# Sliding-window attention and a multiplicative feed-forward network on one core: two weight matrices multiplied on chip, and an attention of one key block per query block, placed by hand

## The chip, the core and the metric

One core of a Trainium2 chip runs the whole program. The metric is the device time of one execution in microseconds (us), as the median of several runs. Engines are named as the profile names them: PE (TensorE; PEld are its weight loads), DVE (VectorE), ACT (ScalarE), POOL (GpSimd) and SP (SyncE). Each engine works through its own instructions in order and waits on semaphores for the others.

## What is computed

```python
B, H, S, D = 8, 8, 576, 64
scores = (1 / sqrt(D)) * q @ k.transpose(0, 1, 3, 2)       # q, k, v: [B, H, S, D]
rel = pos[:, None] - pos[None, :]
# heads 0 to 3 ("plain"):   0 <= rel < 32
# heads 4 to 7 ("dilated"): 0 <= rel < 128 and rel % 4 == 0
attn = softmax(scores where the head's mask holds)
x = (attn @ v).transpose(0, 2, 1, 3).reshape(4608, 512)
a = x @ w1; b = x @ w2                                      # w1, w2: [512, 1024]
out = ((a * b) @ w3) @ w_out                                # w3: [1024, 1024], w_out: [1024, 512]
```

All inputs and the output are float32 in HBM; the kernels convert to bf16 in the load and multiply in bf16.

## The kernel before

The text of the kernel runs through the batches (`attention_batch(b)`), and then through nine blocks of 512 tokens (`ffn_block(t)`). The order on the chip is another: the framework's scheduler reorders what is independent, and so sets feed-forward matmuls of early blocks between the attention of later batches.

Attention of one batch: q, k and v are loaded by POOL's DMA queue with rows of 64 elements, v twice (`ve` and `vo`, the second shifted by 64 rows), so that each of these DMAs consists of some 4600 short pieces. Two heads at a time are copied together by DVE (`qp`, L220), turned by PE in five 128x128 transposes (`tps`, L223) and copied to `qT2` and `kT2` (L228). Scores are made with keys as the stationary operand: each block of 128 keys (K = 64 rows of the array) meets up to 256 queries (L241), 1024 columns a head. ACT takes the exponential (L249, L252), DVE multiplies with a 0/1 mask (L256). For each block of 128 queries, the probabilities are the stationary operand and v the moving one (L278, 65 columns; the last column of ones gives the sum), two key blocks are accumulated, DVE takes the reciprocal (L286) and multiplies (L287), PE transposes (L297) and DVE copies to `XT` (L303), which holds x transposed for all tokens.

Feed-forward of one block: for each of 8 column groups f, four matmuls of 512 columns into `a_ps` (L316) and four into `b_ps` (L324), one PSUM buffer each; ACT copies `a_ps` (L332), DVE multiplies (L333) into `gt`. Then 64 matmuls with w3 into `h_ps` (L340), each eighth copied by ACT to `ht` (L347), and 32 with w_out into `y_ps` (L354), copied by DVE (L362) and stored by SP (L363). The weights come in 24 pieces through POOL's queue (L97), three per batch in the text.

## Time and profile before

| | |
|---|---|
| median of 3 runs | 497.8 us (495.61 to 499.69) |
| span of the profiled execution, first to last instruction | 494.6 us |
| its own time | not given beside its span; the median lies 3.2 us above the span |
| PE busy | 439.3 us (89%) |
| DVE, ACT, POOL busy | 223.7, 176.8, 78.9 us (45%, 36%, 16%) |
| mean granted TensorE clock | 0.983 of full speed |

The profile is one execution. Busy times are the union of an engine's instructions. Matmuls are pipelined, so the duration of one is longer than its distance to the next; distances of starts are what a row of many costs.

### The profile page before, as it was taken

To read this page: it belongs to the slowest core of one execution; us is meant where nothing else is said; L and a number is where in the kernel's file an instruction comes from. 1 tells how busy PE (TensorE), PEld (TensorE's weight loads), DVE (VectorE), ACT (ScalarE), POOL (GpSimd) and SP (SyncE) were. 2 spreads that over 40 slices of the span, in tenths; PEclk is the share of its full clock that TensorE was granted. 3 is DMA by queue.
4 is the path that set the end of the run, shared out by engine and by line. 5 is a ranking of instruction groups with operands and counts; after the bars stand their busy time and mean duration, and the time that the engine had idled before them with its cause. 6 is when DMAs were issued, how large, how long until landed. Compare 5 with 4: busy or idle time off the path is not lost.

```text
span 494.6 us, 6953 instructions
## 1 busy us (share of the span) xinstructions
PE 439.3 (89%) x2816; PEld 211.2 (43%) x2816; DVE 223.7 (45%) x533; ACT 176.8 (36%) x336; POOL 78.9 (16%) x84
## 2 busy tenths in 40 slices
PE   0166799879989989989989999999999999999996
PEld 0033444334544534545535545444444444444442
DVE  0375477246757547766577755321311312302302
ACT  1054074147065254264444471222231231331320
POOL 7542162151050240230300000000000000000000
PEclk9999999799999989999999999999999999999999
DMA  9999599699299098096790000200101101002002
GB/s 102 162 154 166 63 144 188 116 100 93 86 125 67 3 147 108 25 147 44 48 111 24 1 1 8 79 0 24 63 1 42 42 1 64 23 0 86 0 1 85
DMA packets 156255, 33.93 MB, mean 69 GB/s; under 512 B 148544, under 2 KB 149568, under 8 KB 156224
## 3 DMA queue, kind: packets, MB, share of 16 engines
q0 software_dynamic: 151040, 24.06, 82.6%
q1 hardware_dynamic: 5184, 9.44, 5.1%
q8 instruction: 22, 0.36, 0.3%
q14 instruction: 9, 0.07, 0.0%
HBM read 48.10 MB, written 9.44 MB: 116 GB/s over the span
## 4 chain that ended last, share of the span: by engine, by line
PE 66%; issue 14%; DMA 11%; POOL 4%; DVE 3%; ACT 1%; DVEq 0%; POOLq 0%
PE h_ps L340 22%; PE b_ps L324 11%; PE y_ps L354 11%; PE a_ps L316 10%; DMA vo<-in_v_dram 7%; PE o_ps L278 3%; DMA w_sb<-in_moe_w_dram 2%; PE sA L241 2%; PE tps L223 2%; DMA qn<-in_q_dram 2%; PE sB L241 2%; PE x_ps L297 1%; POOL kn L176 1%; POOL ve L183 1%; POOL vo L187 1%
## 5 line engine op out<-in xcount | busy, mean ns | idle before, releaser
L340 PE MATMUL h_ps<-gt,w_sb 128*128 128x512 bf16 x576 | 143.1, 386 | 2.5 <-DMA w_sb<-in_moe_w_dram 2.4
L332 ACT CAST a_sb<-a_ps 128x512 bf16<-128x512 f32 x72 | 42.2, 586 | 141.5 <-PE a_ps L316 137.6
L324 PE MATMUL b_ps<-XT,w_sb 128*128 128x512 bf16 x288 | 80.6, 381 | 0.9 <-DVE gt L333 0.9
L316 PE MATMUL a_ps<-XT,w_sb 128*128 128x512 bf16 x288 | 80.1, 384 | 0.2 <-ACT a_sb L332 0.2
L347 ACT CAST ht<-h_ps 128x512 bf16<-128x512 f32 x72 | 42.3, 588 | 104.9 <-PE h_ps L340 104.9
L340 PEld LDWEIGHTS <-w_sb 128*128 128x128 bf16 x576 | 53.1, 99 | 59.5 <-DMA w_sb<-in_moe_w_dram 3.9
L333 DVE TENSOR_TENSOR gt<-b_ps,a_sb 128x512 bf16<-128x512 f32 x72 | 49.7, 690 | 50.8 <-PE b_ps L324 49.5
L354 PE MATMUL y_ps<-wo_sb,ht 128*128 128x512 bf16 x288 | 70.9, 386 | 0.0
L362 DVE COPY o_sb<-y_ps 128x512 f32<-128x512 f32 x36 | 24.8, 689 | 96.3 <-PE y_ps L354 93.9
L256 DVE TENSOR_TENSOR et<-et,maskpk 128x1024 bf16<-128x1024 bf16 x64 | 43.9, 685 | 26.0 <-ACT et L252 13.8
L249 ACT ACTIVATE et<-sA 128x512 bf16<-128x512 f32 x64 | 38.8, 607 | 32.6 <-PE sA L241 31.9
L278 PEld LDWEIGHTS <-et 128*128 128x128 bf16 (+1 forms) x576 | 30.7, 106 | 35.3 <-DVE et L256 19.1
L241 PEld LDWEIGHTS <-kT 64*128 64x128 bf16 x320 | 24.8, 100 | 49.0 <-DVE kT L228 26.0
L223 PE MATMUL tps<-ident,qp 128*128 128x128 bf16 x320 | 31.5, 235 | 15.9 <-POOL ident masks.py:199 12.6
L278 PE MATMUL o_ps<-ve,et 128*128 128x65 bf16 (+1 forms) x288 | 31.1, 204 | 12.3 <-DVE et L256 9.2
L324 PEld LDWEIGHTS <-w_sb 128*128 128x128 bf16 x288 | 26.9, 97 | 35.0 <-issue 12.4
L241 PE MATMUL sA<-qT,kT 64*128 64x256 bf16 x128 | 27.2, 297 | 14.0 <-DVE kT L228 14.0
L354 PEld LDWEIGHTS <-ht 128*128 128x128 bf16 x288 | 26.8, 99 | 29.0 <-issue 1.7
L252 ACT ACTIVATE et<-sB 128x512 bf16<-128x512 f32 x64 | 38.6, 604 | 1.1 <-PE sB L241 0.7
L316 PEld LDWEIGHTS <-w_sb 128*128 128x128 bf16 x288 | 26.8, 98 | 27.6 <-issue 1.5
L223 PEld LDWEIGHTS <-qp 128*128 128x128 bf16 x320 | 23.3, 104 | 27.1 <-issue 9.8
L287 DVE TENSOR_TENSOR xo<-o_ps,rcp 128x256 bf16<-128x256 f32 (+1 forms) x80 | 33.7, 422 | 2.4
(49 smaller groups left out, 291.9 us busy)
## 6 DMA issues: line engine op xcount, KB each, us to landing
out_dram<-o_sb SPq DMA_DIRECT2D x36, 256.0 KB, 2.0
qn<-in_q_dram POOLq DMA_DIRECT2D x8, 576.0 KB, 11.1
kn<-in_k_dram POOLq DMA_DIRECT2D x8, 576.0 KB, 9.5
ve<-in_v_dram POOLq DMA_DIRECT2D x8, 576.0 KB, 8.4
vo<-in_v_dram POOLq DMA_DIRECT2D x8, 560.0 KB, 11.8
w_sb<-in_moe_w_dram POOLq DMA_DIRECT2D x16, 256.0 KB, 11.8
wo_sb<-in_moe_w_out_dram POOLq DMA_DIRECT2D x8, 128.0 KB, 7.0
vo<-in_v_dram POOLq DMA_DIRECT2D x8, 8.0 KB, 10.1
```

Source lines behind the costliest of these rows:

```text
L223: nc.tensor.transpose(out=tps[:, P * a : P * (a + 1)], in_=qp[:, a, :, :], identity=ident,)
L241: nc.tensor.matmul(out=dstps[:, o0 : o0 + NQ[j]], lhsT=kT2[prt, col0 : col0 + P], rhs=qT2[prt, col0 : col0 + NQ[j]], start=True, stop=True,)
L249: nc.scalar.activation(out=et[:, 0:HALF], in_=sA, func=ACT.Exp, scale=scale)
L256: nc.vector.tensor_tensor(out=et, in0=et, in1=mask, op=AL.mult)
L278: nc.tensor.matmul(out=o_ps[0:nq, hl, 0 : D + 1], lhsT=lhsT, rhs=rhs, start=(ji == 0), stop=(ji == len(js) - 1),)
L316: nc.tensor.matmul(out=a_ps[:, 0:tn], lhsT=w1_sb[:, cch, f * P : (f + 1) * P], rhs=XT[:, cch, t0 : t0 + tn], start=(cch == 0), stop=(cch = ...
L324: nc.tensor.matmul(out=b_ps[:, 0:tn], lhsT=w2_sb[:, cch, f * P : (f + 1) * P], rhs=XT[:, cch, t0 : t0 + tn], start=(cch == 0), stop=(cch = ...
L332: nc.scalar.copy(out=a_sb[:, 0:tn], in_=a_ps[:, 0:tn])
L333: nc.vector.tensor_tensor(out=gt[:, f, 0:tn], in0=b_ps[:, 0:tn], in1=a_sb[:, 0:tn], op=AL.mult)
L340: nc.tensor.matmul(out=h_ps[:, 0:tn], lhsT=w3_sb[:, f, g * P : (g + 1) * P], rhs=gt[:, f, 0:tn], start=(f == 0), stop=(f == KFF - 1),)
L347: nc.scalar.copy(out=ht[:, g, 0:tn], in_=h_ps[:, 0:tn])
L354: nc.tensor.matmul(out=y_ps[0:nr, :], lhsT=ht[:, g, tb * P : tb * P + nr], rhs=wo_sb[:, g, :], start=(g == 0), stop=(g == KFF - 1),)
```

## The change

`out` is computed as (a * b) @ (w3 @ w_out): w3 is transposed on PE (`fuse_t`, 64 transposes), multiplied with w_out on chip (`fuse_m`, 64 matmuls of 512 columns) into `wf_sb`, and each block of 512 tokens then needs 32 matmuls (`ffn2`) in the place of 64 and 32. `ffn1` is the first half, with three PSUM buffers that `a`, `b`, `y` and the fused product share; `y` is copied by ACT.

q and k are loaded with 18 whole rows per partition and turned by DVE (`transposes`, 32x32 blocks of 4-byte pairs), one call for q and one for k per group of four heads; a head then lies on 32 partitions, with even and odd elements of D as the two accumulated halves. Query blocks are 96 queries (plain heads) or 72 queries of one residue mod 4 (dilated heads), and one block of 128 keys holds all that they see. v is loaded in these key blocks: one DMA for the plain heads (`load_vp`) and eight for the dilated ones (`load_vd`). One step is four heads (u = 0 plain, 1 dilated) and half of the queries (hf), so a batch has four steps.

The scheduler is switched off: instructions stand on each engine in the order of the text. Batch 0's attention comes first; that of batches 1 to 7 is cut in 126 pieces ("phases": scores of two heads, values, transposes back), 18 a batch, which `point()` calls between the feed-forward groups by the table `marks`. There is a point ahead of each group of four feed-forward matmuls. Points are counted from 1 to 232; the last phase is called at point 172. A batch's loads are issued when the phases of the batch ahead begin.

The core of the diff (loads, constants and removed lines left out; the second halves of `values` and `xpose` are the same for the dilated heads, with 8 matmuls for each of two residues r and 8 transposes):

```diff
+    ctx.enter_context(tc.manual_schedule())
...
+    qk_pool = ctx.enter_context(tc.tile_pool(name="qk", bufs=2))
+    ps_s = ctx.enter_context(tc.tile_pool(name="pss", bufs=1, space=bass.MemoryType.PSUM))
+    ps_o = ctx.enter_context(tc.tile_pool(name="pso", bufs=1, space=bass.MemoryType.PSUM))
+    ps_x = ctx.enter_context(tc.tile_pool(name="psx", bufs=1, space=bass.MemoryType.PSUM))
+    ps_f = ctx.enter_context(tc.tile_pool(name="psf", bufs=3, space=bass.MemoryType.PSUM))
+    NET = 3
+    ets = [const.tile([P, ETW], BF16, name=f"et{i}") for i in range(NET)]
+    kts = [const.tile([P, PADK + S, 2], BF16, name=f"kt{i}") for i in range(NKT)]
+    qts = [const.tile([P, S, 2], BF16, name=f"qt{i}") for i in range(NKT)]
...
+    def transposes(b, u):
+        for nm, dst, pad in (("qn", qts[u], 0), ("kn", kts[u], PADK)):
+            t = qk[(nm, b)]
+            nc.vector.transpose(
+                out=dst[:, pad : pad + S, :]
+                .rearrange("p s c -> p (s c)")
+                .bitcast(U32)
+                .rearrange("p (j a) -> p a j", a=ROWS),
+                in_=t[:, u, :].bitcast(U32).rearrange("p (a i) -> p a i", a=ROWS),
+            )
...
+        def scores(self, hp):
+            u, hf = self.u, self.hf
+            if hf == 0 and hp == 0:
+                transposes(self.b, u)
+            qt, kt = qts[u], kts[u]
+            sp = ps_s.tile([P, 2, TB], F32, tag="s", name="sp")
+            if u == 0:
+                blocks = [
+                    (96 * (3 * hf + m), 96 * (3 * hf + m), 96, 96 * m, 1) for m in range(3)
+                ]
+            else:
+                blocks = []
+                for bl in range(4):
+                    r, w = 2 * hf + bl // 2, bl % 2
+                    blocks.append((PADK + 64 * w + r, 288 * w + r, 72, 72 * bl, 4))
+            for k0, q0, nq, c0, st in blocks:
+                for c in range(2):
+                    for g in range(2):
+                        prt = slice(32 * (2 * hp + g), 32 * (2 * hp + g) + 32)
+                        nc.tensor.matmul(
+                            out=sp[:, g, c0 : c0 + nq],
+                            lhsT=kt[prt, k0 : k0 + st * (P - 1) + 1 : st, c],
+                            rhs=qt[prt, q0 : q0 + st * (nq - 1) + 1 : st, c],
+                            start=(c == 0),
+                            stop=(c == 1),
+                        )
...
+            nc.scalar.activation(out=ev, in_=sp[:, :, 0:HALF], func=ACT.Exp, scale=scale)
+            if u == 0:
+                mk = mask_pl[:, hf, :, :].rearrange("p m x -> p (m x)")
+            else:
+                mk = mask_di.rearrange("p r w x -> p (r w x)")
+            nc.vector.tensor_tensor(
+                out=ev, in0=ev, in1=mk.unsqueeze(1).to_broadcast([P, 2, HALF]), op=AL.mult
+            )
+        def norm(self, o, nq, nj, xo):
...
+            nc.vector.reciprocal(out=rcp[0:nq, :, 0:nj], in_=ov[:, :, :, D])
+            nc.vector.tensor_tensor(
+                out=xo[0:nq, :, 0:nj, :],
+                in0=ov[:, :, :, 0:D],
+                in1=rcp[0:nq, :, 0:nj].unsqueeze(3).to_broadcast([nq, 2, nj, D]),
+                op=AL.mult,
+            )
+        def values(self, r=0):
+            o = ps_o.tile([P, 2, TB], F32, tag="o", name="o")
+            self.xo = getattr(self, "xo", {})
+            xo = wk_pool.tile([P, 2, 6, D], BF16, tag="xo", bufs=3, name="xo")
+            self.xo[r] = xo
+            if self.u == 0:
+                vp = vps[self.b % NV]
+                for hp in range(2):
+                    for m in range(3):
+                        for hl in range(2):
+                            h = 2 * hp + hl
+                            j = 2 * m + hl
+                            c0 = h * HALF + 96 * m
+                            nc.tensor.matmul(
+                                out=o[:, hp, j * (D + 1) : (j + 1) * (D + 1)],
+                                lhsT=self.et[:, c0 : c0 + P],
+                                rhs=vp[:, h * 6 + 3 * self.hf + m, 0 : D + 1],
+                                start=True,
+                                stop=True,
+                            )
+                self.norm(o, 96, 6, xo)
+            else:
+                vd = vds[self.b % NV]
+                for hp in range(2):
+                    for w in range(2):
...
+                self.norm(o, 72, 4, xo)
+        def xpose(self):
+            x = ps_x.tile([P, 4 * 2 * P], BF16, tag="x", name="x")
+            tok0 = self.b * S
+            if self.u == 0:
+                xv = x[:, 0 : 2 * HALF].rearrange("p (h t) -> p h t", h=2)
+                for hp in range(2):
+                    for m in range(3):
+                        nc.tensor.transpose(
+                            out=xv[:, hp, 96 * m : 96 * m + 96],
+                            in_=self.xo[0][0:96, hp, 2 * m : 2 * m + 2, :],
+                            identity=ident[0:96, 0:96],
+                        )
+                t0 = tok0 + HALF * self.hf
+                nc.vector.tensor_copy(out=XT[:, 0:2, t0 : t0 + HALF], in_=xv)
+            else:
+                xv = x[:, 0 : 2 * HALF].rearrange("p (r h t) -> p r h t", r=2, h=2)
...
+                dst = XT[:, 2:4, tok0 : tok0 + S].rearrange("p h (t r) -> p r h t", r=4)
+                for r in range(2):
+                    nc.scalar.copy(out=dst[:, 2 * self.hf + r, :, :], in_=xv[:, r, :, :])
+    def batch_phases(bs):
+        steps = []
+        for b in bs:
+            for u in range(2):
+                for hf in range(2):
+                    steps.append(Step(len(all_steps), b, u, hf))
+                    all_steps.append(steps[-1])
+        ph = []
+        prev = None
+        for st in steps + [None]:
+            a = []
+            if st is not None:
+                a.append(lambda st=st: st.scores(0))
+            if prev is not None:
+                a.append(lambda st=prev: st.values(0))
+            if st is not None:
+                a.append(lambda st=st: st.scores(1))
+            if prev is not None:
+                if prev.u == 1:
+                    a.append(lambda st=prev: st.values(1))
+                a.append(lambda st=prev: st.xpose())
+            ph += a
+            prev = st
+        return ph
...
+    def ffn1(t, f, point):
+        t0 = t * TB
+        if f == 0:
+            gts[t] = wk_pool.tile([P, KFF, TB], BF16, tag="gt", bufs=3, name="gt")
+        pss = []
+        for w_sb in (w1_sb, w2_sb):
+            point()
+            ps = ps_f.tile([P, TB], F32, tag="f", name="ab")
+            for c in range(DCH):
+                nc.tensor.matmul(
+                    out=ps,
+                    lhsT=w_sb[:, c, f * P : (f + 1) * P],
+                    rhs=XT[:, c, t0 : t0 + TB],
+                    start=(c == 0),
+                    stop=(c == DCH - 1),
                 )
+            pss.append(ps)
+            if len(pss) == 1:
+                a_sb = wk_pool.tile([P, TB], BF16, tag="asb", bufs=3, name="asb")
+                nc.scalar.copy(out=a_sb, in_=ps)
+        nc.vector.tensor_tensor(out=gts[t][:, f, :], in0=pss[1], in1=a_sb, op=AL.mult)
+    def ffn2(t, tb, point):
+        point()
+        y = ps_f.tile([P, d_model], F32, tag="f", name="y")
         for f in range(KFF):
+            if f == KFF // 2:
+                point()
+            nc.tensor.matmul(
+                out=y,
+                lhsT=gts[t][:, f, tb * P : (tb + 1) * P],
+                rhs=wf_sb[:, f, :],
+                start=(f == 0),
+                stop=(f == KFF - 1),
+            )
+        o_sb = wk_pool.tile([P, d_model], F32, tag="osb", bufs=3, name="osb")
+        nc.scalar.copy(out=o_sb, in_=y)
+        r0 = t * TB + tb * P
+        nc.sync.dma_start(out=out[r0 : r0 + P, :], in_=o_sb)
+    def fuse_t(ft):
+        x = ps_x.tile([P, KFF, P], BF16, tag="x", name="x3")
         for g in range(KFF):
+            nc.tensor.transpose(
+                out=x[:, g, :], in_=w3t[ft][:, g * P : (g + 1) * P], identity=ident
+            )
+        w3T[ft] = wk_pool.tile([P, KFF, P], BF16, tag="w3T", bufs=2, name="w3T")
+        nc.scalar.copy(out=w3T[ft], in_=x)
+    def fuse_m(ft, point):
+        point()
+        ps = ps_f.tile([P, d_model], F32, tag="f", name="wf")
+        for g in range(KFF):
+            if g == KFF // 2:
+                point()
+            nc.tensor.matmul(
+                out=ps,
+                lhsT=w3T[ft][:, g, :],
+                rhs=wo_sb[:, g, :],
+                start=(g == 0),
+                stop=(g == KFF - 1),
+            )
+        nc.vector.tensor_copy(out=wf_sb[:, ft, :], in_=ps)
+    load_qk(0, us=(0,), both=False)
+    build_constants()
+    load_vp(0)
+    load_qk(0, us=(1,), both=False)
+    load_vd(0)
+    for c in range(4):
+        load_w12(c)
+    load_qk(1)
+    load_vp(1)
+    load_vd(1)
+    load_wo()
+    for ft in range(KFF):
+        load_w3(ft)
+    for ph in batch_phases([0]):
+        ph()
+    phases = batch_phases(list(range(1, B)))
+    per = len(phases) / (B - 1)
+    marks = [(0, 0.0), (14, per), (56, 2 * per + 6)]
+    for t in range(3, 8):
+        marks.append((56 + 24 * (t - 2) - 3, per * t))
+    xs = [m[0] for m in marks]
+    ys = [min(m[1], len(phases)) for m in marks]
+    state = {"pt": 0, "done": 0}
+    def point():
+        state["pt"] += 1
+        want = int(np.ceil(np.interp(state["pt"], xs, ys)))
+        while state["done"] < min(want, len(phases)):
+            i = state["done"]
+            phases[i]()
+            state["done"] += 1
+            bb = 1 + int(state["done"] // per) + 1
+            if bb < B and bb not in issued and state["done"] % per >= 1:
+                issued.add(bb)
+                load_qk(bb)
+                load_vp(bb)
+                load_vd(bb)
+    issued = {1}
+    for f in range(KFF):
+        ffn1(0, f, point)
+    for f in range(KFF):
+        ffn1(1, f, point)
+    fuse_t(0)
+    for ft in range(KFF):
+        if ft + 1 < KFF:
+            fuse_t(ft + 1)
+        fuse_m(ft, point)
+    for tb in range(4):
+        ffn2(0, tb, point)
+    for t in range(2, NT):
+        for i in range(4):
+            ffn1(t, 2 * i, point)
+            ffn1(t, 2 * i + 1, point)
+            ffn2(t - 1, i, point)
+    for tb in range(4):
+        ffn2(NT - 1, tb, point)
+    assert state["done"] == len(phases)
```

## Rows read from the trace of the kernel before

**Rows 1.** The page: busy time of each engine, and PE and DMA in 40 slices.

```profile
PE 439.3 (89%) x2816; PEld 211.2 (43%) x2816; DVE 223.7 (45%) x533; ACT 176.8 (36%) x336; POOL 78.9 (16%) x84
...
PE   0166799879989989989989999999999999999996
...
DMA  9999599699299098096790000200101101002002
```

**Rows 2.** The chain in order of time, us 327 to 352: start, us, what.

```profile
327.35 13.81 PE h_ps L340 x64
341.16 6.91 PE y_ps L354 x32
...
349.80 0.86 PE a_ps L316 x4
350.66 1.01 PE b_ps L324 x4
```

**Rows 3.** Timeline of PE: start, us, line, operation (shapes) and count, idle before.

```profile
209.20 0.44 PE L223 MATMUL tps<-ident,qp 128*128 128x128 bf16 x5
209.48 0.59 PE L316 MATMUL a_ps<-XT,w_sb 128*128 128x512 bf16 x2
...
212.28 0.38 PE L316 MATMUL a_ps<-XT,w_sb 128*128 128x512 bf16 x1
212.60 0.39 PE L241 MATMUL sA<-qT,kT 64*128 64x256 bf16 x2
212.92 0.39 PE L316 MATMUL a_ps<-XT,w_sb 128*128 128x512 bf16 x1
...
300.37 0.23 PE L278 MATMUL o_ps<-vo,et 128*128 128x65 bf16 x2
300.43 0.22 PE L278 MATMUL o_ps<-ve,et 128*128 128x65 bf16 x2
```

**Rows 4.** Groups by line and shape: count, busy us, mean ns, idle before.

```profile
L333 DVE TENSOR_TENSOR gt<-b_ps,a_sb 128x512 bf16<-128x512 f32 x72 | 49.7, 690 | 50.8 <-PE b_ps L324 49.5 <-DMA vo<-in_v_dram 1.2
L256 DVE TENSOR_TENSOR et<-et,maskpk 128x1024 bf16<-128x1024 bf16 x64 | 43.9, 685 | 26.0 <-ACT et L252 13.8 <-issue 9.3 <-ACT a_sb L332 2.8
L347 ACT CAST ht<-h_ps 128x512 bf16<-128x512 f32 x72 | 42.3, 588 | 104.9 <-PE h_ps L340 104.9
...
L249 ACT ACTIVATE et<-sA 128x512 bf16<-128x512 f32 x64 | 38.8, 607 | 32.6 <-PE sA L241 31.9
...
L287 DVE TENSOR_TENSOR xo<-o_ps,rcp 128x256 bf16<-128x256 f32 x64 | 27.1, 423 | 1.9
```

**Rows 5.** Timeline of the start: what the first loads release.

```profile
8.98 0.49 DVE L220 COPY qp<-qn 128x640 bf16<-128x640 bf16 x1 [7.91 <-DMA qn<-in_q_dram]
...
12.23 0.33 POOL masks.py:199 TENSOR_SCALAR_AFFINE_SELECT ident<-ident 128x128 bf16<-128x128 bf16 x1
...
12.76 0.49 DVE L220 COPY qp<-kn 128x640 bf16<-128x640 bf16 x1 [3.29 <-DMA kn<-in_k_dram]
...
17.66 0.09 DVE L197 MEMSET ve<- 128x36 bf16 x1 [3.47 <-DMA ve<-in_v_dram]
```

**Rows 6.** Timeline of POOL, us 82 to 85: loads of 256 KB one by one.

```profile
82.95 0.53 POOL L97 DMA_DIRECT2D wo_sb<-in_moe_w_out_dram  x1 [0.71 <-DMA w_sb<-in_moe_w_dram]
84.23 0.53 POOL L97 DMA_DIRECT2D wo_sb<-in_moe_w_out_dram  x1 [0.76 <-DMA w_sb<-in_moe_w_dram]
```

**Rows 7.** PE's longest waits (timeline), and stretches with granted clock (windows).

```profile
109.18 0.20 PE L278 MATMUL o_ps<-ve,et 128*128 128x65 bf16 x1 [2.61 <-DVE et L256]
...
179.54 0.20 PE L278 MATMUL o_ps<-ve,et 128*128 128x65 bf16 x1 [2.10 <-DVE et L256]
...
216.52 0.20 PE L278 MATMUL o_ps<-ve,et 128*128 128x65 bf16 x1 [2.08 <-DVE et L256]
...
109.40:112.90 3.50, 3.50 (x16) 1.40 (x14) 1.90 (x6) 2.30 (x4) 1.72 (x1) 0.51 3.51 141
...
181.10:188.00 6.90, 6.90 (x35) 3.04 (x32) 2.83 (x8) 3.89 (x8) 1.81 (x1) 0.51 2.62 156
```

**Rows 8.** Timeline of the end: the last work before the span closes.

```profile
490.76 0.69 DVE L362 COPY o_sb<-y_ps 128x512 f32<-128x512 f32 x1 [1.03 <-PE y_ps L354]
```

More of the change, by code (lines that the diff above doesn't have):

```diff
@@ L13 @@
 F32 = mybir.dt.float32
-I32 = mybir.dt.int32
+U32 = mybir.dt.uint32
 AL = mybir.AluOpType
@@ L19 @@
 DILATION = 4
-NQ = [256, 256, 256, 192, 64]
-OFF = [0, 256, 512, 768, 960]
-ETW = 1024
-HALF = 512
+S = 576
+D = 64
+ROWS = 18
+HALF = 288
+PADK = 32
+PITCH = 80
+ETW = 4 * HALF + 64
+TB = 512
 @with_exitstack
@@ new lines @@
+    wo_sb = const.tile([P, KFF, d_model], BF16, name="wo_sb")
+    wf_sb = const.tile([P, KFF, d_model], BF16, name="wf_sb")
+    XT = const.tile([P, DCH, n_tok], BF16, name="XT")
+    ident = const.tile([P, P], BF16, name="ident")
+    mask_pl = const.tile([P, 2, 3, 96], BF16, name="mask_pl")
+    mask_di = const.tile([P, 2, 2, 72], BF16, name="mask_di")
+    NV = 2
+    vps = [const.tile([P, 24, PITCH], BF16, name=f"vp{i}") for i in range(NV)]
+    vds = [const.tile([P, 4, 2, 4, PITCH], BF16, name=f"vd{i}") for i in range(NV)]
@@ new lines, with load_qk @@
+    NET = 3
+    ets = [const.tile([P, ETW], BF16, name=f"et{i}") for i in range(NET)]
+    NKT = 2
+    kts = [const.tile([P, PADK + S, 2], BF16, name=f"kt{i}") for i in range(NKT)]
+    qts = [const.tile([P, S, 2], BF16, name=f"qt{i}") for i in range(NKT)]
+    qk = {}
+    def load_qk(b, us=(0, 1), both=True):
+        for nm, src in (("qn", q), ("kn", k)):
+            if (nm, b) not in qk:
+                qk[(nm, b)] = qk_pool.tile([P, 2, ROWS * D], BF16, tag=nm, name=nm)
+            t = qk[(nm, b)]
+            flat = src[b].rearrange("(u h) s d -> u (h s d)", u=2)
+            if both:
+                nc.gpsimd.dma_start(
+                    out=t, in_=flat.rearrange("u (p x) -> p u x", p=P)
+                )
+            else:
+                for u in us:
+                    nc.gpsimd.dma_start(
+                        out=t[:, u, :], in_=flat[u].rearrange("(p x) -> p x", p=P)
+                    )
@@ new lines, in load_vp, with src @@
+    def load_vp(b):
+        vp = vps[b % NV]
+        base = v[b, 0, 0, 0:1]
+        off = base.offset
+        def src(p0, n, j0, nj):
+            return bass.AP(
+                tensor=base.tensor,
+                offset=off + (96 * j0 - 32 + p0) * D,
+                ap=[[D, n], [96 * D, nj], [1, D]],
+            )
+        if b == 0:
+            nc.gpsimd.dma_start(out=vp[32:P, 0:1, 0:D], in_=src(32, 96, 0, 1))
+            nc.gpsimd.dma_start(out=vp[:, 1:24, 0:D], in_=src(0, P, 1, 23))
+        else:
+            nc.gpsimd.dma_start(out=vp[:, :, 0:D], in_=src(0, P, 0, 24))
@@ new lines, in load_vd, with load_w12 @@
+    def load_vd(b):
+        vd = vds[b % NV]
+        for h in range(4):
+            for w in range(2):
+                nc.gpsimd.dma_start(
+                    out=vd[:, h, w, :, 0:D],
+                    in_=v[b, 4 + h, 64 * w : 64 * w + 512, :].rearrange(
+                        "(p r) d -> p r d", r=4
+                    ),
+                )
+    def load_w12(c):
+        for dst, src in ((w1_sb, moe_w1), (w2_sb, moe_w2)):
+            nc.gpsimd.dma_start(
+                out=dst[:, :, 256 * c : 256 * (c + 1)],
+                in_=src[:, 256 * c : 256 * (c + 1)].rearrange("(a p) f -> p a f", p=P),
+            )
@@ L365 @@
-    for b in range(B):
-        attention_batch(b)
-    issue_weight_chunks(len(weight_chunks))
-    for t in range(n_tblk):
-        ffn_block(t)
+        for t in ets:
+            nc.gpsimd.memset(t[:, 4 * HALF : ETW], 0.0)
+        for t in kts:
+            nc.gpsimd.memset(t[:, 0:PADK, :], 0.0)
+        for t in vps:
+            nc.gpsimd.memset(t[:, :, D : D + 1], 1.0)
+        for t in vds:
+            nc.gpsimd.memset(t[:, :, :, :, D : D + 1], 1.0)
+        nc.gpsimd.memset(vps[0][0:32, 0:1, 0:D], 0.0)
```

359 lines of the change are left out of this document (69 added, 290 removed).

## The prediction

> **What bounds the kernel now.** I read the page first. PE is busy for 439 of 494.6 us, and in tenths it stands at 8 or 9 from the fourth slice (37 us) to the end; no other engine passes 45%. The first three slices are the exception: PE shows 0, 1 and 6 while the DMA engines are full [rows 1]. So there are two stages: a start that waits for loads and for the first batch's chain, and then a PE that hardly waits. In the second the chain in order of time is PE alone, one group after another [rows 2]. What changes PE's work there changes the time one for one; what changes DVE or ACT only does so if it makes PE wait. A busy PE need not be efficient, so I took prices from distances of starts: 64 matmuls of 512 columns take 13.81 us, 0.216 each [rows 2]; five 128-column transposes 0.28, 0.056 each; two value matmuls of 65 columns 0.06, 0.031 each. Scores use 64 rows of the array, and the change of form costs: a 512-column matmul ahead of them takes 0.32 in the place of 0.216, and two of 256 columns ahead of a full one 0.32 in the place of 0.22, so 0.2 us for there and back [rows 3].
>
> **Feed-forward (removed and added, all on PE's path).** One block costs 35.6 us now: 8 times 0.86 + 1.01, then 13.81 and 6.91 [rows 2]; nine blocks 320. After: 64 matmuls of the first half 13.81, 32 of the second 6.91, nine times 20.72 = 186.5. The 0.15 in the 1.01 (`b` waits for its only PSUM buffer) goes too, since three buffers give an evacuation of 0.59 or 0.69 [rows 4] two groups (1.7 us) of room. The product on chip adds 13.81 + 64 x 0.056 = 17.4. Sum 204; gain 116 us.
>
> **Attention on PE.** Before, a batch is 40 transposes (2.2), 8 x 1024 score columns (3.4), 72 value matmuls (2.2) and 20 transposes (1.1): 9 us and the form changes. After it is 112 score matmuls, 56 value matmuls and 28 transposes. At 0.42 ns a column (0.216/512): plain scores 48 x 0.040, dilated 64 x 0.031, eight form changes 1.6, values 1.7, transposes 1.0: 8.2 us. So fewer scores are made that the mask drops, but PE's time is about the same. Seven batches are 57; two phases are counted with the start: 55. Two things no row shows. Neighbouring score matmuls lie on different 32-row strips and may run side by side: lower bound half their columns, 42 in all. The dilated ones read queries and keys 16 bytes apart: upper bound 0.11 each, the price of a 256-column one [rows 3], which adds 5.1 us a batch, 91 in all. I take 55, since every row of the trace streams at the one rate.
>
> [...]
>
> **The start.** Now q of batch 0 lands ahead of 8.98, k 3.8 us later, v 4.9 after that, each 576 KB in short pieces [rows 5]; the weights with long pieces take 1.27 us per 256 KB [rows 6]. After, q and k of four heads are long pieces: 2 x 1.4 us from about 3.7, so 6.5. POOL then builds masks and ones ahead of all other loads; its select over 128 columns takes 0.33 [rows 5], and some 15 instructions with up to 576 columns I put at 6.6 us, so the plain v is issued at 9 and lands by 14.5, the other q and k by 17.3, the dilated v by 21.7 (4096 short pieces at v's rate), w1 and w2 by 31.9 (2 MB), q and k of batch 1 (1.1 MB) by 37.6. Batch 0's attention has nothing beside it: 18 phases, each a chain of PE, ACT 0.65, DVE 0.45 or more; I get 33 us for its end. But the first `point()` stands ahead of the first feed-forward matmul and calls two score phases of batch 1. PE, in order, waits there for q and k of batch 1, two transposes, two scores and an exponential: feed-forward starts at 41 us (36 if constants and chunk rate are hidden; 48 if q and k go at 3.8 us per 576 KB and constants take double).
>
> **New waits.** DVE works at about 1.04 ns an element plus 0.16 (0.690 for 512, 0.423 for 256 [rows 4]). (1) `transposes` stands in DVE's queue directly ahead of the scores that need it, 576 4-byte elements, 0.76 each, 1.5 for q and k. From the fourth block on the point lies in the middle of a `y` group: DVE ends the last `gt` 0.9 us after its matmuls, then 1.5, while PE has only 0.86 of work: PE waits 1.55, and everything behind, feed-forward too, waits with it. Nine such; by their places in the list of points three others cost 2.4 to 2.6 and one 0.5: 22 us. No row shows a DVE transpose; the 0.45 of a packed one and double, 1.35, are my bounds, and I take the price of the rows with one element a step. (2) The second value phase of a dilated step is followed after one group (0.86) by its transposes back, which need a reciprocal and a 0.69 multiplication that stand behind a mask and a `gt`: about 1.2 and 0.4 a batch, 11 us. (3) The first block has 18 phases at 14 points, and batch 2's q and k land (behind w_out and w3, 25 us of loads) about when they are wanted: 7. Sum 40, bounds 20 and 70. ACT (8 exponentials, 4 copies a batch, `a`, `y`) stays near 130 us and DVE near 165, both below PE; POOL issues loads one batch ahead, which hides them.
>
> **Clock.** PE has five waits of 1.9 to 2.6 us (three stand in the rows). Two were followed by 3.5 and 6.9 us at half the granted clock (2.61 at 109.18, 2.10 at 179.54), that of 2.08 at 216.52 was not [rows 7]. A fall loses half its length. With some four waits above 2 us I add 4 (0 to 14).
>
> **Sum.** 41 + 204 + 55 + 40 + 4 and a tail of 4 (the last copy at 490.76, end at 494.6 [rows 8]; ACT does it now, 0.59) give a span of 348, and the median lies 3.2 above the profiled span: 351 us, 0.71 of before. The gain is the product of weights (116), the start's overlap and little else: attention's price on PE is about the same, and the hand-set order gives some 40 back.
>
> **Rivals.** (A) Score matmuls of two strips overlap and DVE transposes are quick: 36 + 204 + 42 + 20 + 0 + 4 + 3 = 309; half of it 330. For it: the strips and PSUM banks of each pair differ; against: no row has two matmuls side by side. [...] (B) PE pays for stride, or DVE for its strided transposes: 351 + 36 = 387 at the upper bound of the one, 381 with all waits at 70, 417 with both. For it: the 16-byte steps; against: nothing in the trace. [...] (D) The change doesn't do what it says, because the loads and not the phases set the pace: batch 2's loads 10 us later than I think, and each further batch as late, would add 10 to 30 (360 to 380); it falls in the range of the forecast.
>
> **How the numbers follow.** Forecast with its own errors, 330 to 378: 0.58, with D in it. A, 305 to 330: 0.16. B, 378 to 417: 0.23. C: 0.02. Other ways to no change: 0.01. Half of A and half of B lie outside 317 to 396, so that is the range. The measurement of before spreads by 0.8%, so 1% is about what tells a change from none. Faster by more than 1% are all but C and the last: 0.97; same 0.01, slower 0.02.
>
> **What would show it.** Feed-forward groups of four at 0.86 us and 64 fewer matmuls of 512 columns a block; the first `ab` matmul near 41 us, released by a DMA of batch 1; PE idle before `sp` ended by the DVE transpose, 13 times about 1.5 us, and before `x` ended by DVE's `xo`; after point 172, PE without waits for the last 50 us. Wrong would make it: score matmuls of the dilated heads far from 0.031 us apart, a DVE transpose far from 0.76, PE waiting for loads after the first block, or granted clock below 0.9 in the middle.

## The result and the profile after

The changed kernel takes 390.92 us as the median of 4 runs (390.43 to 391.96), the kernel before 496.71 beside it: a ratio of 0.786, 95% interval 0.7824 to 0.7893. The forecast was 351, the range 317 to 396. The profiled execution has a span of 389.0 us against a forecast of 348, so there are 41 us to explain. The time lies in the range, but only 5 us from its upper end. In the run with packed transposes below, one of the four executions took 716 us and is the one profiled: its time is left out, and only single DVE instructions are read from its profile.

The page after, against [rows 1] (busy time of the engines, then PE, granted clock and DMA in 40 slices):

```profile
PE 314.3 (81%) x2516; PEld 166.6 (43%) x2560; DVE 171.7 (44%) x288; ACT 135.9 (35%) x213; POOL 87.4 (22%) x131
...
PE   0382768887887989987987979697969798899995
...
PEclk9999989796997998999896989798988899999998
DMA  3999999996600579009920977072000000111103
```

PE is still the only engine above half, yet from the 21st to the 32nd slice every second digit of its row is a 6 or 7, and the clock row has dips there too. The slices behind, where attention ends (the last scores start at 322 us), have neither. By stages (us; busy time and instructions of PE, PEld, DVE, ACT, POOL; granted clock; DMA share; GB/s):

```profile
0.00:42.00 42.00, 15.51 (x221) 12.07 (x223) 17.92 (x29) 10.30 (x15) 30.07 (x57) 1.00 1.29 145
42.00:384.70 342.70, 298.70 (x2296) 154.49 (x2338) 153.76 (x259) 124.97 (x198) 57.37 (x75) 0.91 0.51 74
384.70:389.00 4.30, 0.04 (x1) 0.00 (x0) 0.00 (x0) 0.58 (x1) 0.00 (x0) 0.77 0.28 109
```

Start and tail are as forecast (41 and 4); the miss lies in the middle, where the mean granted clock is 0.91. The timeline of PE and of DVE shows one period of it (start, us, what, idle before):

```profile
39.59 0.66 PE L215 MATMUL sp<-qt,kt 32*128 32x96 bf16 x12 [6.34 <-DVE kt L183]
...
41.99 1.49 PE L350 MATMUL ab<-XT,w_sb 128*128 128x512 bf16 x3 [0.33 <-issue]
...
193.72 1.27 PE L215 MATMUL sp<-qt,kt 32*128 32x72 bf16 x16
194.93 1.04 PE L369 MATMUL y<-wf_sb,gt 128*128 128x512 bf16 x4
...
203.65 0.38 PE L350 MATMUL ab<-XT,w_sb 128*128 128x512 bf16 x1 [0.87 <-ACT XT L309]
203.87 1.02 PE L369 MATMUL y<-wf_sb,gt 128*128 128x512 bf16 x4
...
204.07 0.69 DVE L361 TENSOR_TENSOR gt<-ab,asb 128x512 bf16<-128x512 f32 x1 [2.30 <-PE ab L350]
204.68 1.25 DVE L183 STREAM_TRANSPOSE qt<-qn 128x576 uint32<-128x576 uint32 x1
205.76 1.24 DVE L183 STREAM_TRANSPOSE kt<-kn 128x576 uint32<-128x576 uint32 x1
...
207.06 0.66 PE L215 MATMUL sp<-qt,kt 32*128 32x96 bf16 x12 [2.17 <-DVE kt L183]
207.65 1.89 PE L369 MATMUL y<-wf_sb,gt 128*128 128x512 bf16 x4
```

The first two lines are the forecast start: scores of batch 1 wait for its keys, and the first `ab` comes at 41.99. From 203.65 on stands a wait as forecast, `gt`, `qt`, `kt` one behind another on DVE while PE has one group of four, but longer: 2.17 us. Behind it four `y` matmuls take 1.89 us in the place of 1.02: the granted clock, 1.00 of full speed from 190 to 205 us, is 0.50 from 208 to 212 ("half clock" from here on). PE's waits ahead of `sp` that end with `kt` are 12 after 42 us, 26.4 us in all, seven of them of 2.17 to 2.38 at 182, 205, 224, 246, 265, 287 and 306. The granted clock stands at 0.50 in 12 pieces of 3.4 or 6.8 us after 42 us, 61.4 us in all; seven of them begin during or just behind those seven waits. The windows of three of the pieces, columns as above, against the two in [rows 7]:

```profile
90.10:96.90 6.80, 6.56 (x40) 3.30 (x41) 2.25 (x5) 1.24 (x2) 1.58 (x3) 0.50 0.94 170
120.80:127.60 6.80, 6.31 (x39) 3.38 (x40) 2.34 (x5) 1.66 (x2) 0.00 (x0) 0.50 0.00 0
...
308.50:311.90 3.40, 3.40 (x30) 1.79 (x25) 0.64 (x2) 1.24 (x2) 0.00 (x0) 0.50 0.02 5
```

In the 12 pieces PE is busy for 55.7 us; half of that, 28 us, is an estimate of what the clock costs. It is rather 26: 4.2 us of the 55.7 are dilated score phases, which take no longer at half clock (1.22 us, below). The groups by shape (busy us, mean ns, idle before):

```profile
L215 PE MATMUL sp<-qt,kt 32*128 32x72 bf16 x512 | 41.0, 314 | 19.4 <-DVE kt L183 19.0 <-ACT et L225 0.2
L215 PE MATMUL sp<-qt,kt 32*128 32x96 bf16 x384 | 17.3, 234 | 27.4 <-DVE kt L183 25.0 <-ACT et L225 2.2
...
L309 ACT COPY XT<-x 128x288 bf16<-128x288 bf16 x32 | 23.1, 852 | 14.5 <-PE x L302 14.5
L390 ACT COPY w3T<-x 128x1024 bf16<-128x1024 bf16 x8 | 8.1, 1012 | 10.5 <-PE x L386 10.5
L183 DVE STREAM_TRANSPOSE qt<-qn 128x576 uint32<-128x576 uint32 x16 | 20.0, 1249 | 8.2 <-DMA qn<-in_q_dram 8.2
```

Dilated and plain scores have equally many columns (512 x 72 and 384 x 96), and the dilated ones keep PE busy for 41.0 us against 17.3. From start to the next group's start a dilated phase of 16 takes 1.21 us (193.72 to 194.93), a plain one of 12 takes 0.37. The DVE transpose takes 1.25 us, forecast 0.76.

### The profile page after: what moved, and what is told of

The parts are those of the page before. It is cut to its first block, busy times and chain, and to the rows that moved or that the text cites. A ratio compares the mean times of both kernels' runs of the same rounds, so it can differ in the third digit from the quotient of the medians.

```text
span 389.0 us, 6039 instructions
## 1 busy us (share of the span) xinstructions
PE 314.3 (81%) x2516; PEld 166.6 (43%) x2560; DVE 171.7 (44%) x288; ACT 135.9 (35%) x213; POOL 87.4 (22%) x131
## 5 line engine op out<-in xcount | busy, mean ns | idle before, releaser
L350 PE MATMUL ab<-XT,w_sb 128*128 128x512 bf16 x548 | 151.2, 406 | 9.1 <-ACT XT L309 6.4
L215 PE MATMUL sp<-qt,kt 32*128 32x72 bf16 (+1 forms) x896 | 58.3, 279 | 46.9 <-DVE kt L183 44.0
L350 PEld LDWEIGHTS <-w_sb 128*128 128x128 bf16 x576 | 53.2, 103 | 63.0 <-issue 17.8
L225 ACT ACTIVATE et<-sp 128x576 bf16<-128x576 f32 x64 | 41.8, 653 | 100.9 <-PE sp L215 100.9
L124 POOL DMA_DIRECT2D vd<-in_v_dram x64 | 47.2, 743 | 130.3 <-PE o L274 109.2
L215 PEld LDWEIGHTS <-kt 32*128 32x128 bf16 x896 | 43.5, 128 | 74.4 <-DVE kt L183 43.6
L369 PE MATMUL y<-wf_sb,gt 128*128 128x512 bf16 x275 | 74.2, 403 | 1.1 <-issue 0.8
L361 DVE TENSOR_TENSOR gt<-ab,asb 128x512 bf16<-128x512 f32 x72 | 49.6, 689 | 57.6 <-PE ab L350 56.6
L360 ACT CAST asb<-ab 128x512 bf16<-128x512 f32 x72 | 42.1, 585 | 72.7 <-PE ab L350 61.5
L238 DVE TENSOR_TENSOR xo<-o,rcp 72x512 bf16<-72x512 f32 (+1 forms) x48 | 37.2, 775 | 1.7
```

Of the source, the lines that this page charges most:

```text
L124: nc.gpsimd.dma_start(out=vd[:, h, w, :, 0:D], in_=v[b, 4 + h, 64 * w : 64 * w + 512, :].rearrange("(p r) d -> p r d", r=4),)
L215: nc.tensor.matmul(out=sp[:, g, c0 : c0 + nq], lhsT=kt[prt, k0 : k0 + st * (P - 1) + 1 : st, c], rhs=qt[prt, q0 : q0 + st * (nq - 1) + 1 : ...
L225: nc.scalar.activation(out=ev, in_=sp[:, :, 0:HALF], func=ACT.Exp, scale=scale)
L238: nc.vector.tensor_tensor(out=xo[0:nq, :, 0:nj, :], in0=ov[:, :, :, 0:D], in1=rcp[0:nq, :, 0:nj].unsqueeze(3).to_broadcast([nq, 2, nj, D]) ...
L350: nc.tensor.matmul(out=ps, lhsT=w_sb[:, c, f * P : (f + 1) * P], rhs=XT[:, c, t0 : t0 + TB], start=(c == 0), stop=(c == DCH - 1),)
L360: nc.scalar.copy(out=a_sb, in_=ps)
```

## The experiments

Each expectation numbers its own theories. Two come back in the text. The theory of the waits (the first of the run with early transposes): the two DVE transposes, standing directly ahead of the scores that need them, cause PE's waits of 2.2 us, and these waits let the granted clock fall. The theory of the phases (the third of the run without the step): it is the dilated score phases of 1.21 us that let it fall. All times are beside runs of the kernel before on the same chip (medians of 497 to 499 us). Time at half clock leaves out a piece in the tail of each run.

**Transposes one step earlier.** The transposes of a later step's q and k are called in the step ahead, one at each score call; batch 0 and the first of batches 1 and 2 stay in place.

```diff
+    in_place = {(0, 0), (0, 1), (1, 0), (2, 0)}
...
-            if hf == 0 and hp == 0:
+            if hf == 0 and hp == 0 and (self.b, u) in in_place:
                 transposes(self.b, u)
+            nxt = (self.b, 1) if u == 0 else (self.b + 1, 0)
+            if hf == 1 and nxt not in in_place and nxt[0] < B:
+                transposes(*nxt, which=(hp,))
```

> DVE turns q during the first score phase of the step before, and k during the second, for all groups but the first three; nothing else is moved. In the changed kernel 12 waits of PE behind these transposes are 26 us, and 11 falls of the granted clock are 61 us at half clock. Theory 1 (the waits are what lets the clock fall): waits and nearly all falls go, 391 - 24 - 26 = 341 us, granted clock above 0.97. Theory 2 (the clock falls for what PE does in the short matmuls, not for the waits): the falls stay, 391 - 24 = 367 us, clock about 0.92. Theory 3 (the 1.25 us pieces on DVE only move the wait to the gt multiplication and its PSUM buffer): 380 to 391 us.

346.28 us, ratio 0.6966 (0.6932 to 0.7), near the 341 of the theory of the waits. Windows and PE's waits:

```profile
120.00:200.00 80.00, 77.73 (x705) 41.05 (x705) 47.40 (x80) 35.77 (x58) 24.19 (x32) 1.00 0.79 103
...
PE sp L221 <- DVE kt L184: 22.4, 4, 8.4
PE ab L356 <- ACT XT L315: 7.0, 8, 0.9
```

Of the 15 waits for `kt` four are left, three of them in batch 0 and ahead of the first `ab`, the fourth (4.85 us at 64) behind batch 2's loads. One fall of 6.8 us is left, beside that wait; the dilated phases are as slow as before. Nothing was made quicker: PE has the same matmuls, and DVE the same transposes. 45 us went with the place of 24 DVE instructions: 21.5 of them are PE's waits, and the estimate above gives 24 for the clock.

**Dilated scores without the step.** Rows 16 bytes apart are replaced by neighbouring ones, 4 bytes apart, so other positions are multiplied; counts, shapes and order stay.

```diff
-    blocks.append((PADK + 64 * w + r, 288 * w + r, 72, 72 * bl, 4))
+    blocks.append((PADK + 64 * w + r, 288 * w + r, 72, 72 * bl, 1))
```

> The dilated heads' scores read 128 neighbouring keys and 72 neighbouring queries in the place of every fourth, as many columns and matmuls as before (so these scores are of other positions than the reference's). Theory 1 (the 16-byte step costs PE): a dilated score phase falls from 1.21 us to about 0.6, as the plain one: 28 phases x 0.6 = 17 us, 391 - 17 = 374 us, with the falls of the clock left as they are. Theory 2 (the pairs of weight loads of 32 rows set the pace, not the step): 1.2 us stays, 391 us. Theory 3 (these slow phases are what the clock falls for): 391 - 17 - 26 = 348 us.

358.8 us, ratio 0.7225 (0.7183 to 0.7267). Timeline of PE:

```profile
177.38 0.45 PE L215 MATMUL sp<-qt,kt 32*128 32x72 bf16 x16
177.76 1.90 PE L350 MATMUL ab<-XT,w_sb 128*128 128x512 bf16 x8
...
192.51 0.43 PE L215 MATMUL sp<-qt,kt 32*128 32x96 bf16 x12 [2.17 <-DVE kt L183]
```

From start to start the phase now takes 0.38 us. 28 phases after the start, at 0.83 less each, are 23 us of the 32. The seven waits of 2.2 us all stay, and still only 27 us are at half clock, 61 before: two of the seven are followed by a fall (10 us), where all seven were (34 us). So the theory of the waits alone isn't enough, nor that of the phases: in the late batches the wait is the occasion (without it, with early transposes, the granted clock is 1.00 from 120 us on), and the slow phases beside it decide how often it is followed by one.

**The framework's order.** One line less; the phases and `point()` stay in the text, the scheduler places them.

```diff
-    ctx.enter_context(tc.manual_schedule())
```

> The changed kernel with the framework's scheduler on again, nothing else. Theory 1 (the hand-set order is what makes PE wait behind the transposes, and the clock falls for that): the scheduler moves them ahead, 340 to 360 us. Theory 2 (the single PSUM buffers of scores and values make the waits in any order): 385 to 400 us. Theory 3 (the hand-set order is what keeps PE fed): above 400 us.

339.03 us, ratio 0.6844 (0.6789 to 0.6899). The page's slices of PE and clock:

```profile
PE   0486898489999999999998999999899999999994
...
PEclk9999997959999999999999999999999999999999
```

The first `ab` starts at 23.9 us instead of 42.0, PE waits for `kt` only once, for 9.3 us ahead of the first scores, and 13.7 us are at half clock. The hand-set order costs 52 us against the framework's.

**The product alone.** The kernel before, with w3 @ w_out made once and its own attention and order kept.

```diff
-        ht = ht_pool.tile([P, KFF, TB], BF16, tag="ht")
...
-                    lhsT=ht[:, g, tb * P : tb * P + nr],
-                    rhs=wo_sb[:, g, :],
+                    lhsT=gt[:, g, tb * P : tb * P + nr],
+                    rhs=wf_sb[:, g, :],
...
+        nc.scalar.copy(out=w3T, in_=x_ps)
+        wf_ps = ps_hy.tile([P, d_model], F32, tag="hy")
+        for g in range(KFF):
+            nc.tensor.matmul(
+                out=wf_ps, lhsT=w3T[:, g, :], rhs=wo_sb[:, g, :],
+                start=(g == 0), stop=(g == KFF - 1),
+            )
+        nc.vector.tensor_copy(out=wf_sb[:, ft, :], in_=wf_ps)
```

> The kernel before with one part of the change alone: w3 @ w_out multiplied on chip, 32 second-half matmuls a block in the place of 96. Theory 1 (attention's part of the change brings nothing, as its PE time says): 497 - 116 = 381 us. Theory 2 (with a third less feed-forward work to lay between, the old attention's own chain and loads, which end near 305 us in the kernel before, set the time): 410 to 450 us, with PE waiting in the first 300 us.

400.09 us, ratio 0.8051 (0.7984 to 0.8119): 97 of the 116 us counted for it, between the two theories. The clock row of the page and PE's waits:

```profile
PEclk9999999997978996998699959978999999999999
...
PE sA L243 <- DVE kT L230: 18.0, 7, 11.7
...
PE o_ps L280 <- DVE et L258: 8.3, 6, 2.7
PE wf_ps L368 <- DMA wo_sb<-in_moe_w_out_dram: 4.5, 1, 4.5
```

What is missing is mostly clock. PE has six waits of 1.6 to 2.7 us for attention and `gt`, where before had five of 1.9 to 2.6, and 4.5 us for w_out; but 47.8 us are at half clock, where before had 17 (three pieces of 6.8, 3.4 and 6.8). PE is busy for 46.2 and 16.4 us of these, so by the estimate above some 15 of the missing 19 us go with the clock. The rest of the change, attention with its order, is worth 400 - 391 = 9 us as it was built, and 400 - 339 = 61 us under the scheduler.

**DVE transposes with a packed output.** The output's step of 72 bytes becomes one of 4, so other positions are multiplied; the score matmuls keep their steps.

```diff
-                .rearrange("p (j a) -> p a j", a=ROWS),
+                .rearrange("p (a j) -> p a j", a=ROWS),
```

> The changed kernel, with the DVE transposes writing their output in one packed run in the place of 72-byte steps (queries and keys then stand in another order, so the scores are of other positions than the reference's). Theory 1 (the step of the output is what makes them 1.25 us in the place of the 0.76 forecast): 0.76 each, PE's waits fall from 2.2 to 1.2 us, and with these shorter waits most falls of the clock go: 391 - 12 - 20 = about 359 us; if the falls stay, 379. Theory 2 (a transpose of 4-byte elements takes 1.25 us for 576 in any order): 391 us.

365.5 us as the median of three, ratio 0.7316 (0.726 to 0.7373). DVE's groups in its profile, where `gt` takes 691 ns against 689 in the changed kernel:

```profile
L183 DVE STREAM_TRANSPOSE qt<-qn 128x576 uint32<-128x576 uint32 x16 | 12.3, 769 | 10.0 <-DMA qn<-in_q_dram 10.0
L183 DVE STREAM_TRANSPOSE kt<-kn 128x576 uint32<-128x576 uint32 x16 | 11.8, 740 | 3.7 <-DMA kn<-in_k_dram 3.7
```

That is the forecast's price of 0.76. Two instructions shorter by 0.5 us each should make 12 waits shorter by 1 us; the other half of the 25 us would then go with the clock (a mean of 0.965 to 0.974 in these three, 0.918 after). This division is worked out and not read from a trace.

**Which operand.** Only the keys (weights; first diff), or only the queries (moving; second diff), keep the 16-byte step; the other operand reads neighbouring rows, so other positions are multiplied.

```diff
-    rhs=qt[prt, q0 : q0 + st * (nq - 1) + 1 : st, c],
+    rhs=qt[prt, q0 : q0 + nq, c],
```

```diff
-    lhsT=kt[prt, k0 : k0 + st * (P - 1) + 1 : st, c],
+    lhsT=kt[prt, k0 : k0 + P, c],
```

> Dilated scores with every fourth key (the stationary operand) and neighbouring queries (scores of other positions than the reference's). If the weight loads are what the 16-byte step slows, a dilated score phase stays at 1.2 us and the time at 391; if the moving operand is, it falls to 0.4 and the time to 359, as in the run with neither stepped; if both, in between.

> The other half: neighbouring keys and every fourth query (scores of other positions than the reference's). If the moving operand is what the 16-byte step slows, the phase stays at 1.2 us and the time at 391; if the weight loads are, it falls to 0.4 and the time to 359.

One execution each: 369.1 and 386.1 us. Timeline, first the kernel with stepped keys:

```profile
183.60 0.69 PE L215 MATMUL sp<-qt,kt 32*128 32x72 bf16 x16
184.22 1.04 PE L369 MATMUL y<-wf_sb,gt 128*128 128x512 bf16 x4
```

and the one with stepped queries:

```profile
188.32 1.20 PE L215 MATMUL sp<-qt,kt 32*128 32x72 bf16 x16
189.45 1.90 PE L350 MATMUL ab<-XT,w_sb 128*128 128x512 bf16 x8
```

From start to start the phase takes 0.62 and 1.13 us (1.21 with both, 0.38 with neither). The moving operand pays most: its step adds 0.75 us, that of the weights 0.24, and only 0.08 beside stepped queries. Nor does the granted clock change the price. In the changed kernel the whole of this stretch lies in the piece at half clock from 90.1 us:

```profile
90.34 1.28 PE L215 MATMUL sp<-qt,kt 32*128 32x72 bf16 x16 [3.10 <-DVE kt L183]
91.56 3.59 PE L350 MATMUL ab<-XT,w_sb 128*128 128x512 bf16 x8
```

The phase takes 1.22 us, as at full clock, while the `ab` matmuls behind it cost twice as much as at full clock. With stepped queries alone it is 1.13 at either level; without a step it is 0.38 to 0.40 at full clock and 0.6 at half (the latter in the run by residue below, at 53.45 and 56.92 us).

The two runs also fill in the falls behind the seven late waits: 34 us at half clock with phases of 1.21 us, 27 with 1.13, 20 with 0.62 (six of the seven waits in both), 10 with 0.38.

**By residue, under the scheduler.** The whole computation, with the step moved into the load: q and k of dilated heads come by residue in pieces of one row, and the DVE transposes set the residues side by side (second cut), so the matmuls read neighbours.

```diff
+                rows = flat[1].rearrange("(h a j d) -> h j a d", h=4, a=ROWS, d=D)
+                for h in range(4):
+                    nc.gpsimd.dma_start(
+                        out=t[32 * h : 32 * (h + 1), 1, :].rearrange(
+                            "p (a d) -> p a d", a=ROWS
+                        ),
+                        in_=rows[h],
+                    )
...
+                    .rearrange("p (r a j) -> p a j r", r=4, a=ROWS),
...
-                    blocks.append((PADK + 64 * w + r, 288 * w + r, 72, 72 * bl, 4))
+                    blocks.append(
+                        (PADK + 144 * r + 16 * w, 144 * r + 72 * w, 72, 72 * bl, 1)
+                    )
```

> The full computation, scheduler on, and q and k of the dilated heads loaded in short pieces (row 32a + j on partition j) so that the transposes set the residues side by side and scores read without a step. Theory of the two prices (steps and hand order): 339 less 28 x 0.8 = 317 us, as long as the 9216 more short pieces of load a batch pair hide behind the work; if they show at the start, 5 us are given back: 322. If the step's price had only been hidden by other waits under the scheduler: 335 to 340.

322.3 us, ratio 0.6463 (0.6416 to 0.6509), 17 less than the scheduler's version with the step. POOL is busy for 126 us with the short pieces, 87 before that; from 100 us on PE hides it (busy for 97 of the next 100 us). Windows:

```profile
40.00:60.00 20.00, 15.95 (x201) 10.10 (x198) 13.93 (x24) 6.97 (x11) 11.21 (x18) 0.75 1.45 163
60.00:80.00 20.00, 17.43 (x92) 8.05 (x92) 10.26 (x17) 8.14 (x13) 15.44 (x22) 0.83 1.76 165
80.00:100.00 20.00, 17.04 (x210) 11.29 (x209) 14.39 (x24) 9.08 (x13) 18.45 (x26) 0.74 1.82 141
...
120.00:200.00 80.00, 77.80 (x791) 38.62 (x788) 51.93 (x91) 38.52 (x64) 35.17 (x49) 1.00 1.11 121
```

All 27 us at half clock lie between 49.9 and 97.7 us, in two pieces. The last weight lands at 66.5 us, so the second piece (from 87.4) lies behind the loading of weights; from 83.9 to 93.2 us PE has attention and one feed-forward matmul there, and no wait above 0.81 us. The 322 of the expectation came out, but not by its start: the first `ab` comes at 25.2 us against 23.9, and the time at half clock grew from 13.7 to 27 us.

**The first phases later, by hand.** The order of the first experiment, with no phase ahead of point 4.

```diff
-    marks = [(0, 0.0), (14, per), (56, 2 * per + 6)]
+    marks = [(3, 0.0), (16, per + 2), (56, 2 * per + 6)]
```

> The hand-set order with the transposes one step ahead (346 us in the run of that name), and the first feed-forward points left without a phase: batch 1's scores are no longer called ahead of the first feed-forward matmul, but at the fourth point. In the trace of the change PE waits 6.3 us at 33 to 40 us for batch 1's keys while XT of batch 0 is ready at about 35. If that place in the list is a price of its own, the first `ab` starts near 35 us and the time is 340 us (338 to 342). If the first block is paced by its phases anyway (18 phases then stand at fewer points, each one closer behind the one before), what is won at the start is lost in the first 40 us of feed-forward: 345 to 348.

345.44 us, ratio 0.695 (0.6919 to 0.698), against 0.6966: no difference shown. The first `ab` starts at 33.5 us, 8 earlier, but the wait for batch 2's keys grows from 4.85 to 7.50 us, and half clock from 6.8 to 17.1. The second expectation holds: what was won at the start is lost by 74 us.

**By residue, by hand.** The same with the loads by residue.

> The same order, and queries and keys of the dilated heads laid out by residue, so that no score matmul steps by 16 bytes (28 dilated phases, each 0.8 us shorter). If the place of the transposes, the first points and the step are all that the hand-set order costs against the framework's scheduler, this kernel meets the scheduler's by-residue version (322 us): 318 to 324. If the order has a further price, or if the short pieces of the loads by residue are late in the hand-set order, it stays at 328 us or more.

331.21 us, ratio 0.6662 (0.6636 to 0.6689): a further price, as the second half of the expectation has it. PE's waits:

```profile
PE sp L248 <- DVE kt L209: 26.2, 3, 11.8
```

One wait of 11.8 us at 62: batch 2's q and k land at 66.7 to 72.9, in POOL's queue behind w_out and w3.

**Batch 2 ahead of w3.** Only the order of POOL's loads is changed (in the text, batch 0's phases, whose buffers batch 2 takes over, now stand ahead of them).

```diff
...
+    load_qk(2)
+    load_vp(2)
+    load_vd(2)
     load_wo()
     for ft in range(KFF):
         load_w3(ft)
...
-    issued = {1}
+    issued = {1, 2}
```

> The hand-set order by residue (331 us), and on POOL batch 2's queries, keys and values issued ahead of w_out and w3 rather than behind them. In the run by residue PE's last long wait is one of 11.8 us at 62 us, for batch 2's keys, whose loads land at 66 to 73 us behind 25 us of w_out and w3; 13.7 us at half clock follow it. If that place in POOL's queue is what still lies between the hand-set order and the scheduler's, the wait goes, half clock shrinks by some 10 us, and the time is 312 to 318 us. If w3 is then late for the product, or the attention of the first block, packed more closely, lets the clock fall for longer, it is 322 to 330.

320.77 us, ratio 0.6438 (0.639 to 0.6485). PE's waits:

```profile
PE sp L248 <- DVE kt L209: 18.4, 3, 8.3
```

The wait at 62 is 2.6 us now, half clock 17.1 (23.9); 10 us came back, where 13 to 19 were expected; the wait for batch 1's keys, which ends at 44 us, grew from 6.0 to 7.5. The hand-set order now stands level with the scheduler's (322.3; the intervals overlap).

**XT copies split.** The scheduler's version by residue, every second copy of dilated heads on DVE.

```diff
-    nc.scalar.copy(out=dst[:, 2 * self.hf + r, :, :], in_=xv[:, r, :, :])
+    cp = nc.scalar.copy if r == 0 else nc.vector.tensor_copy
+    cp(out=dst[:, 2 * self.hf + r, :, :], in_=xv[:, r, :, :])
```

> The by-residue version under the framework's scheduler (322 us), and the second of each two copies of dilated heads into XT, 852 ns each on ACT with an output step of 8 bytes, made on DVE. In that version PE waits 7.7 us for ACT's copies ahead of `ab`. If these waits are on the path, 315 to 318 us; if DVE is then the later one, or the waits have another work behind them, 321 to 325.

323.0 us, ratio 0.6499 (0.647 to 0.6527): nothing gained. PE's waits:

```profile
PE ab L377 <- DVE XT L336: 9.0, 9, 1.7
```

DVE's copies to `XT`, with an 8-byte output step here, and packed in the changed kernel:

```profile
L336 DVE COPY XT<-x 128x288 bf16<-128x288 bf16 x16 | 12.8, 797 | 13.7 <-ACT XT L336 13.7
L296 DVE COPY XT<-x 128x576 bf16<-128x576 bf16 x16 | 7.3, 457 | 3.3 <-PE x L290 2.8
```

The wait changed its name, from 7.7 us behind ACT to 9.0 behind DVE. On DVE too the step is dear: half the elements take 1.7 times as long.

## Why the prediction was right in sign and 40 us short

**Start, feed-forward, tail.** 41 forecast, 42.0 measured, for the reason given (the first point calls scores of batch 1, and PE waits in order). The counted 204 us hold: groups of four at 0.86 to 0.87 us. Tail 4, measured 4.3. Of the prediction's four signs of being wrong two came out (a dilated phase far from its price, the transpose far from 0.76); the clock in the middle, 0.91, stands just above its 0.9, and PE does not wait for loads after the first block.

**Clock: the term that failed.** The prediction took "some four waits above 2 us" and added 4 us (0 to 14) from the falls in [rows 7]. Measured: 12 pieces, 61.4 us, an estimated 26 to 28 us lost, 22 to 24 more than the term. The error has two causes. The transposes took 1.25 us each and not 0.76, so seven waits forecast at 1.55 became 2.2; and what stands beside the waits is not before's dense 512-column work but score phases nearly twice as long as priced (1.21 for 0.68). Making the transposes earlier (one cause away) left 6.8 us at half clock, taking the step out (the other) left 27. The second is a matter of degree: phases of 0.62, shorter than priced, still left six falls behind the seven waits. And neither is the whole: falls between 39 and 98 us are left in both of the best versions, without stepped phases. In the hand-set one they stand beside waits of 7.5 and 2.6 us for keys; in the scheduler's no wait from 40 us on is longer than 1.1 us, and no run here isolates what sets those off.

**Waits.** Forecast 40: the transposes' share of 22 was 26.4 (12 waits rather than 13), and all waits above 0.85 us after the start make 36 (PE's whole idle time there is 44). Place and cause were right for the transposes. The 11 us put on `xo` were too much (7.2 ahead of `x` in all), and 6.4 ahead of `ab` behind ACT's copies to `XT` were not foreseen: with an 8-byte output step one of 288 elements takes 852 ns, where a packed one of 1024 takes 1012. The 0.76 came from rows with a packed output [rows 4]; packed, the transpose takes 0.74 to 0.77, and its 72-byte output step makes the difference.

**Attention on PE.** Forecast 55. Distances of starts give 28 x 1.21 for dilated and 26 x 0.37 for plain score phases (two are counted with the start), 12 for values and 7 for transposes: 63. What remains of the 342.7 us beside 204, the clock's 26 to 28 and the idle 44 is 67 to 69; the other 4 to 6 I can't assign. Of the "two things no row shows" both came true, with opposite signs: the dilated phases cost 15 us more than priced, the plain ones 8 less. The dilated phases are rival B: 1.21 where 0.48 + 0.2 was taken, since "every row of the trace streams at the one rate" was a statement on packed operands. With a 16-byte step a phase took 1.21 us (both operands), 1.13 (the moving one) or 0.62 (the weights), against 0.38 without. The plain phases are rival A: 0.37 with both changes of form, where 0.68 was forecast. In the trace the two matmuls of a pair, on neighbouring strips, start 3 ns apart and the next pair 44 ns after them (medians at full clock); one alone has 96 columns, 40 ns at the forecast's 0.42, so a pair takes little more than one.

**The conclusion drawn from the sum.** "The product of weights, the start's overlap and little else" fails. The product alone gave 97 us, since half clock in before's order then grew from 17 to 47.8 us. The new attention is worth 61 us under the scheduler; its first feed-forward matmul comes at 23.9 us, with the product alone at 56.4. And "the hand-set order gives some 40 back" was 52. An order set by hand need not cost anything: with three places of it changed (transposes a step ahead, the first points, batch 2 ahead of w3) and the loads by residue it reaches 320.8 us, 0.82 of the change as built. That kernel and the scheduler's by residue (322.3) beat both kernels compared here.

**Rivals B, C and D.** That 391 lies 4 us from B's 387 is luck. B's sum puts 36 us on the step in PE's own time; measured, the dilated phases cost 15 more than priced, the plain ones take 8 of them back, and the clock, for which B has only the forecast's 4, brings 22 to 24 more. C, slower than before, would have needed 146 us more than the forecast; the clock took an estimated 26 to 28: from 42 us to the last scores at 322 it stood at half for 61 of 280 us, 22%. D's mechanism, loads late for a batch, did not show in the changed kernel: batch 2's q and k land at 64.4 and 67.0 us, ahead of their transposes at 66.3 and 67.4, and after 42 us no transpose waits for a load. It came out only when the rest was tighter: 4.85 us with early transposes, 11.8 us in the hand-set version by residue.

## What to carry to other kernels

Where an order is written by hand, put what another engine must prepare one step ahead of its use (here 391 to 346 us), and read each in-order queue, DMA's included, for who stands in front (here batch 2's q and k behind w_out and w3: a wait of 11.8 us, 2.6 with them ahead). Price an operand by a row with the same step, not by a packed one of the same shape; where none exists, the price is open up to the upper bound (here 1.21 us a phase, between 0.68 as priced and 1.96 at the bound). And add waits of one kind together with what the clock makes of them: here 26 us of waits stood beside 61 us at half clock, and moving their cause gave 45.

## What the runs showed of the hardware that was not expected

- A 16-byte step of a matmul's operands: 16 matmuls of 32 rows and 72 columns take 1.21 us with both stepped, 1.13 with the moving one, 0.62 with the weights, 0.38 with none (4 bytes from element to element). At half clock 1.21 and 1.13 stay as they are, and 0.38 becomes 0.6.
- Two matmuls of 32 rows on neighbouring strips start 3 ns apart: a pair of 96 columns takes 44 ns.
- A DVE transpose of 576 4-byte elements: 1.25 us with an output step of 72 bytes, 0.74 to 0.77 packed.
- An ACT copy of 288 bf16 elements with an 8-byte output step takes 852 ns; the packed copy of 1024 takes 1012 ns. On DVE 288 with the step take 797 ns, 576 packed ones 457.
- Seven waits of 2.2 us were followed by 34 us at half clock with score phases of 1.21 us around them and by 10 us with phases of 0.38.
